# Moving the matmul operands of a three-stage transformer kernel to one address residue in SBUF

## The chip, the cores and the metric

The kernel runs on one core of one Trainium2 chip. The metric is the device time of one execution in microseconds (us). Before the change three runs gave 681.0, 681.89 and 684.74 us; the median is 681.89 us. A kernel computes on four engines with their own instruction queues: TensorE (PE, with its weight loads shown apart as PEld), VectorE (DVE), ScalarE (ACT) and GpSimd (POOL). SyncE (SP) issues the DMAs. SBUF is the on-chip memory from which TensorE reads both operands of a matmul; each of its 128 partitions holds a row of bytes, and "the address" below is the byte offset in that row.

## The reference

Attention with a local window and a few global columns (batch 2, 8 heads, 768 positions, head dimension 64), then two feed-forward stages on the 1536 x 512 result:

```python
scores = where(keep, q @ k.T / sqrt(64) - slope[h] * dist, -1e9)
x = softmax(scores) @ v              # reshaped to 1536 x 512
h = x @ w_in                         # 512 -> 2048
x = (h * cos(h)) @ w_out             # 2048 -> 512
return ((x @ w_a) * (x @ w_b)) @ w_out2   # 512 -> 1536 -> 512
```

The weights come as float64 and are converted on the chip.

## The kernel before

**Matmuls.** Each float32 operand is split into a high and a low part of type fp32r (xTh and xTl, wh and wl, gh and gl, yh and yl, ugh and ugl), and each product is made of three matmuls: high times high, high times low and low times high (lines 669 to 671 for h, a and b; 719 to 721 for y; 766 to 768 for o). Each takes a stationary operand of 128 columns, which a weight load brings into the array (512 bytes per partition), and streams a moving operand of 512 columns through it (2,048 bytes per partition). There are 2,448 such matmuls; the other 1,392 belong to attention (scores, transposes, weighing of v) and are shorter. For h the weights w are stationary and x moves; for y the weights are stationary and g moves; for a and b the weights are stationary and y moves; for o the product ug is stationary and the weights move.

**Stages.** The 1,536 rows are cut into three chunks of 512 (c = 0, 1, 2). Attention runs over 12 tiles of 128 rows, with the h and y work of the finished chunks between them; then h and y go on alone, then a, b and o. The order in which each engine gets its instructions is worked out by a planner (`Plan.order`, line 90) from costs and due times written in the file; it reads no addresses.

**Where tiles lie.** Tiles are allocated one after the other from pools, in this order: `const` (small constants), `keep` (the x and y tiles, and the accumulators acc0 to acc2), `wp` (converted weights, float64 buffers, and u and g tiles), and then `at` for attention, whose room is used afterwards by `post` (more weight and g tiles). Nearly every tile is a multiple of 256 bytes long, so its address modulo 256, the residue below, is that of the tile before it. The exceptions are what the change touches: the constants, which end at 1,856, and the float64 buffers of `RAW_BYTES` = 4,160 bytes (line 23), used in pairs inside the accumulators' room (line 579's `raws`, 2 x 4,160 bytes in each of acc0 to acc2) and singly as raw0 and raw1. The DMA of a weight block lands one byte into such a buffer, so that ScalarE and VectorE can pick bytes out of each float64.

Weight tiles wh and wl live in 17 numbered slots; slot 0 lies before raw0 and raw1, all others behind them.

Of the kernel before, what the change touches and what calls it, by code (L numbers as in the profile page):

```python
# [10 lines left out]
F32 = mybir.dt.float32  # L11
# [8 lines left out]
PSUM = bass.MemoryType.PSUM  # L20

P = 128
RAW_BYTES = 8 * 4 * P + 64
TOP = float(2.0**27)
GLOB = 32
BIG = float(2.0**40)
# [131 lines left out]
def tile_kernel(ctx, tc, q, k, v, n_global, n_local, w_in, w_out, w_a, w_b, w_out2, out):  # L158
# [11 lines left out]
    const = ctx.enter_context(tc.tile_pool(name="const", bufs=1))  # L170
# [41 lines left out]
    low_end = const.tile([P, 1], F32, tag="lowend", name="low_end")  # L212
    other = const.tile([P, 4], F32, tag="other", name="other")
    other_i = const.tile([P, 1], I32, tag="otheri", name="other_i")
    su = keep.tile([P, 2, 4, 2 * P], F32, tag="xh2", name="su")
    su_a, su_b = su[:, 0], su[:, 1]
    d = at.tile([P, H, 2, P], F32, tag="bias", name="bias")
# [340 lines left out]
    def weights():  # L558
        free = [(-1, s) for s in range(N_W[0])] + [(N_PRE, s) for s in range(N_W[0], sum(N_W))]
        free.sort()  # L560
        for n, blk in enumerate(sorted(first, key=lambda b: first[b])):
# [9 lines left out]
            def load(n=n, src=src, idx=idx, tiled=tiled, early=early):  # L571
                if early:
                    if n % 2 == 0:
                        T["raws", n // 2] = keep.tile([P, 2, RAW_BYTES], U8, tag=f"acc{n // 2}", name=f"raws{n // 2}")
                    T["raw", n] = T["raws", n // 2][:, n % 2]
                else:
                    T["raw", n] = wp.tile([P, RAW_BYTES], U8, tag=f"raw{n % 2}", name=f"raw{n}")
                block = src[idx] if tiled else src[idx * P:(idx + 1) * P, :]
# [356 lines left out]
```

## Time and profile before

| | before |
|---|---|
| median of three runs | 681.89 us |
| the profiled execution's own time | 682.8 us |
| its span, first to last instruction | 681.0 us |
| mean granted TensorE clock | 0.99 |
| PE busy / PEld busy | 96% / 79% of the span |
| DVE / ACT / POOL busy | 57% / 52% / 37% |
| 16 DMA engines, share of the span | 22.4% for the one large queue |

The profiled execution is 0.9 us longer than the median, and 1.8 us of its time lie outside the span. A matmul's recorded duration is modelled and overlaps the next matmul, so that the time one really takes is the distance from its start to the start of the next one, read from the timeline. Weight loads are recorded apart; a matmul's own load runs while the matmul before it streams.

### The profile page before, as it was taken

How to read it: one execution, taken by the hardware profiler on the slowest of the kernel's cores; microseconds unless marked ns; L12 is line 12 of the kernel's file. 1: busy time of each engine (PE TensorE's matmuls, PEld its weight loads, DVE VectorE, ACT ScalarE, POOL GpSimd, SP SyncE). 2: the span in 40 equal slices, each digit the busy share in tenths (PEclk: the TensorE clock that was granted, in tenths of full speed). 3: DMA queues.
4: the chain of work that ended last, by engine and by line, in shares of the span. 5: the costliest groups of instructions: out<-in, count | busy, mean ns of one | idle time of the engine just before them, and what ended most of it. 6: DMA issues, size and time to landing. Idle time of an engine off the chain costs nothing.

```text
span 681.0 us, 10027 instructions
## 1 busy us (share of the span) xinstructions
PE 653.7 (96%) x3840; PEld 535.6 (79%) x3840; DVE 388.9 (57%) x731; ACT 354.0 (52%) x621; POOL 253.2 (37%) x232
## 2 busy tenths in 40 slices
PE   3787999999999999999999999999999999999996
PEld 2676778888888888888888888888888888888885
DVE  6988888874877656665475555422552652322243
ACT  4878887866876755766565446411532532111100
POOL 5368773422433533545164235311521422211100
PEclk9988999999999999999999999999999999999999
DMA  7832241311122231213103313200220210000004
GB/s 212 288 88 77 78 127 43 82 42 32 63 93 93 93 124 62 94 63 123 63 31 100 117 36 121 92 1 0 93 92 1 94 62 1 0 1 1 0 34 158
DMA packets 29530, 50.63 MB, mean 74 GB/s; under 512 B 14944, under 2 KB 15776, under 8 KB 29472
## 3 DMA queue, kind: packets, MB, share of 16 engines
q1 hardware_dynamic: 29472, 49.89, 22.4%
q8 instruction: 32, 0.52, 0.3%
q14 instruction: 26, 0.21, 0.1%
HBM read 45.09 MB, written 3.15 MB: 71 GB/s over the span
## 4 chain that ended last, share of the span: by engine, by line
PE 92%; DVE 3%; issue 1%; DMA 1%; ACT 1%; POOL 1%; SPq 0%; DVEq 0%
PE h L669 7%; PE y L719 7%; PE y L721 6%; PE y L720 6%; PE h L670 6%; PE h L671 6%; PE a L670 5%; PE b L670 5%; PE a L669 5%; PE a L671 5%; PE b L671 5%; PE b L669 5%; PE o L767 5%; PE o L768 5%; PE o L766 5%; PE tr L191 3%
## 5 line engine op out<-in xcount | busy, mean ns | idle before, releaser
L194 POOL TENSOR_TENSOR wl<-cv,wh 128x512 fp32r<-128x512 f32 x59 | 79.5, 1351 | 127.8 <-ACT wh L200 127.8
L194 POOL TENSOR_TENSOR ugl<-as,ugh 128x512 fp32r<-128x512 f32 x36 | 47.9, 1331 | 164.5 <-ACT ugh L200 158.0
L754 DVE TENSOR_TENSOR as<-b,as 128x512 f32<-128x512 f32 x36 | 24.9, 691 | 124.6 <-ACT as L200 124.6
L200 ACT ACTIVATE as<-a 128x512 f32<-128x512 f32 x36 | 21.5, 597 | 132.5 <-PE a L671 132.4
L194 POOL TENSOR_TENSOR gl<-u,gh 128x512 fp32r<-128x512 f32 x48 | 64.2, 1353 | 62.7 <-ACT gh L200 57.2
L194 DVE TENSOR_TENSOR cv<-cv,cn 128x512 int32<-128x512 f32 x68 | 59.9, 881 | 32.7 <-ACT cv L586 32.4
L669 PE MATMUL h<-xTh,wh 128*128 128x512 f32 x192 | 76.4, 398 | 0.4 <-DVE u L708 0.4
L719 PE MATMUL y<-gh,wh 128*128 128x512 f32 x192 | 76.2, 397 | 0.0
L670 PE MATMUL h<-xTl,wh 128*128 128x512 f32 x192 | 75.6, 394 | 0.0
L671 PE MATMUL h<-xTh,wl 128*128 128x512 f32 x192 | 75.4, 393 | 0.0
L721 PE MATMUL y<-gh,wl 128*128 128x512 f32 x192 | 75.0, 391 | 0.0
L720 PE MATMUL y<-gl,wh 128*128 128x512 f32 x192 | 74.9, 390 | 0.0
L591 ACT ACTIVATE cn<-raw,low_end 128x512 f32<-128x512 int8 x62 | 47.0, 758 | 22.8 <-DVE cv L194 18.1
L780 DVE TENSOR_TENSOR oacc<-o,oacc 128x512 f32<-128x512 f32 x60 | 41.5, 691 | 27.1 <-PE o L768 26.3
L670 PE MATMUL a<-yl,wh 128*128 128x512 f32 x144 | 56.9, 395 | 0.0
L669 PE MATMUL a<-yh,wh 128*128 128x512 f32 x144 | 56.7, 394 | 0.0
L670 PE MATMUL b<-yl,wh 128*128 128x512 f32 x144 | 56.7, 394 | 0.0
L671 PE MATMUL a<-yh,wl 128*128 128x512 f32 x144 | 56.6, 393 | 0.0
L669 PE MATMUL b<-yh,wh 128*128 128x512 f32 x144 | 56.6, 393 | 0.0
L671 PE MATMUL b<-yh,wl 128*128 128x512 f32 x144 | 56.6, 393 | 0.0
L768 PE MATMUL o<-wh,ugl 128*128 128x512 f32 x144 | 56.3, 391 | 0.0
L767 PE MATMUL o<-wl,ugh 128*128 128x512 f32 x144 | 56.2, 390 | 0.0
(101 smaller groups left out, 1361.1 us busy)
## 6 DMA issues: line engine op xcount, KB each, us to landing
raw<-in_moe_w_out_dram SPq DMA_DIRECT2D x26, 512.0 KB, 3.3
raw<-in_moe_w_in_dram SPq DMA_DIRECT2D x12, 512.0 KB, 3.3
raw<-in_moe_w_a_dram SPq DMA_DIRECT2D x12, 512.0 KB, 3.2
raw<-in_moe_w_b_dram SPq DMA_DIRECT2D x12, 512.0 KB, 3.2
v<-in_v_dram SPq DMA_DIRECT2D x12, 256.0 KB, 3.9
out_dram<-oacc SPq DMA_DIRECT2D x12, 256.0 KB, 2.0
nq<-in_q_dram SPq DMA_DIRECT2D x11, 256.0 KB, 3.4
nk<-in_k_dram SPq DMA_DIRECT2D x11, 256.0 KB, 3.3
```

What stands on the lines that cost most here:

```text
L194: eng.tensor_tensor(out=dst, in0=a, in1=b, op=ALU.subtract)
L591: nc.scalar.activation(out=c, in_=top, func=AF.Relu, bias=low_end, scale=-TOP)
L669: nc.tensor.matmul(dst, wh[:, kk, :], xh[:, kk, :], start=(kk == 0), stop=False)
L670: nc.tensor.matmul(dst, wh[:, kk, :], xl[:, kk, :], start=False, stop=False)
L671: nc.tensor.matmul(dst, wl[:, kk, :], xh[:, kk, :], start=False, stop=(kk == KD - 1))
L719: nc.tensor.matmul(dst, wh[:, m, :], gh, start=(x == 0), stop=False)
L720: nc.tensor.matmul(dst, wh[:, m, :], gl, start=False, stop=False)
L721: nc.tensor.matmul(dst, wl[:, m, :], gh, start=False, stop=(x == L1[g] - 1))
L766: nc.tensor.matmul(dst, uh[:, us], wh, start=(x == 0), stop=False)
L767: nc.tensor.matmul(dst, uh[:, us], wl, start=False, stop=False)
L768: nc.tensor.matmul(dst, ul[:, us], wh, start=False, stop=(x == L2[g] - 1))
L780: nc.vector.tensor_tensor(out=acc, in0=T[inst], in1=acc, op=ALU.add)
```

## The change

Two lines give each buffer another size; no instruction is added, removed or moved. In the built programs each engine has the same instructions in the same order with the same waits, and only the addresses (and the length of a row in the raw buffers) differ.

```diff
-RAW_BYTES = 8 * 4 * P + 64
+RAW_BYTES = 8 * 4 * P + 256
...
     other = const.tile([P, 4], F32, tag="other", name="other")
     other_i = const.tile([P, 1], I32, tag="otheri", name="other_i")
+    const.tile([P, 8], F32, tag="pad", name="pad")
```

What this does to the addresses, read from the two built programs (address modulo 256):

```
tiles                                   before     after
xTh, yh of chunk 2 (tag xh2)              64         96
accumulators 0, 1, 2 (and raws)       64,192,64      96
xTh, yh of chunks 0, 1; xTl, yl of all   192         96
cv, cn; wh and wl of slot 0              192         96
raw0, raw1                             192, 0        96
wh and wl of slots 1 to 16                64         96
u, t, g, ug (high and low)                64         96
attention: kx 64, qT 96 and 160, sp 0, 160 and 192, pt 32 and 224:
                                 each 32 more; ident stays at 128
```

So before, a matmul's moving and stationary operands are either at the same residue (64 and 64, or 192 and 192) or 128 apart (64 and 192); counted over the built program, 1,076 of the 2,448 wide matmuls have their own two operands 128 apart. After, all 2,448 have both at 96, which is 32 modulo 64.

## Rows read from the trace of the kernel before

**Rows 1.** The page: busy shares, 40 slices, chain that ended last.

```profile
PE 653.7 (96%) x3840; PEld 535.6 (79%) x3840; DVE 388.9 (57%) x731; ACT 354.0 (52%) x621; POOL 253.2 (37%) x232
...
PE   3787999999999999999999999999999999999996
...
PEclk9988999999999999999999999999999999999999
...
PE 92%; DVE 3%; issue 1%; DMA 1%; ACT 1%; POOL 1%; SPq 0%; DVEq 0%
```

**Rows 2.** Busy time by stretch: us and instructions; PEclk is the granted clock.

```profile
core 0: us, PE busy (x) PEld busy (x) DVE busy (x) ACT busy (x) POOL busy (x), PEclk, DMA share, GB/s
153.10:674.50 521.40, 521.40 (x2269) 425.65 (x2268) 264.17 (x366) 236.42 (x381) 171.09 (x128) 1.00 0.18 62
...
60.00:153.00 93.00, 91.88 (x1075) 76.24 (x1073) 75.45 (x212) 74.73 (x142) 49.91 (x55) 1.00 0.26 72
```

**Rows 3.** PE's groups in 153.1 to 674.5: xcount | busy us, mean ns | idle before.

```profile
L719 PE MATMUL y<-gh,wh 128*128 128x512 f32 x164 | 64.0, 390 | 0.0
L721 PE MATMUL y<-gh,wl 128*128 128x512 f32 x164 | 63.9, 390 | 0.0
...
L670 PE MATMUL h<-xTl,wh 128*128 128x512 f32 x160 | 63.0, 394 | 0.0
...
L670 PE MATMUL a<-yl,wh 128*128 128x512 f32 x144 | 56.9, 395 | 0.0
...
L768 PE MATMUL o<-wh,ugl 128*128 128x512 f32 x143 | 55.9, 391 | 0.0
```

**Rows 4.** Timeline of PE: start us, duration us; first matmul of successive runs.

```profile
343.32 0.39 PE L719 MATMUL y<-gh,wh 128*128 128x512 f32 x1
...
359.64 0.40 PE L669 MATMUL b<-yh,wh 128*128 128x512 f32 x1
...
362.43 0.40 PE L669 MATMUL a<-yh,wh 128*128 128x512 f32 x1
...
365.23 0.40 PE L669 MATMUL b<-yh,wh 128*128 128x512 f32 x1
...
368.03 0.40 PE L669 MATMUL a<-yh,wh 128*128 128x512 f32 x1
```

**Rows 5.** Timeline of PE, two runs of h of 12 matmuls, y between them.

```profile
285.57 0.39 PE L669 MATMUL h<-xTh,wh 128*128 128x512 f32 x1
...
288.30 0.39 PE L719 MATMUL y<-gh,wh 128*128 128x512 f32 x1
...
291.02 0.40 PE L669 MATMUL h<-xTh,wh 128*128 128x512 f32 x1
291.03 0.19 PEld L670 LDWEIGHTS h<-xTl,wh 128*128 128x128 f32 x1
...
293.82 0.39 PE L719 MATMUL y<-gh,wh 128*128 128x512 f32 x1
```

**Rows 6.** Timeline, the last run of o and what follows it.

```profile
647.62 0.39 PE L766 MATMUL o<-wh,ugh 128*128 128x512 f32 x1
...
674.59 0.39 PE L768 MATMUL o<-wh,ugl 128*128 128x512 f32 x1
675.02 0.69 DVE L780 TENSOR_TENSOR oacc<-o,oacc 128x512 f32<-128x512 f32 x1 [0.67 <-PE o L768]
```

**Rows 7.** Tiles sp, qT, wh, nk and raw: durations min/median/max in ns.

```profile
L191 PEld LDWEIGHTS tr<-ident,sp x176: 137/141/230, 13.1 to 148.3; 128*128 128x128 f32 x176
...
L378 PEld LDWEIGHTS sc<-kx,qT x288: 182/185/336, 6.0 to 133.2; 64*128 64x128 f32 x144
...
L669 PEld LDWEIGHTS h<-xTh,wh x192: 186/188/192, 62.5 to 342.4; 128*128 128x128 f32 x192
...
L197 POOL TENSOR_SCALAR kx<-nk x9: 614/618/623, 9.9 to 120.8; 128x512 fp32r<-128x512 f32 x9
...
L586 ACT ACTIVATE cv<-raw,low_end x62: 734/752/774, 75.0 to 578.4; 128x512 f32<-128x512 int8 x62
```

**Rows 8.** Timeline of PE: one run over v in attention.

```profile
130.80 1.40 PE L426 MATMUL o<-v,pt 128*128 128x65 bf16 x40
132.04 0.52 PE L191 MATMUL tr<-ident,sp 128*128 128x128 f32 x3
```

## The prediction

> **What bounds the kernel now.** I began with the page [rows 1]. PE is busy for 96% of the span, its slices stand at 9 from the fifth of the forty to the last but one, and the chain that ended last is PE for 92%: the reader should see that from there on the kernel lasts as long as PE takes to get through its matmuls. The granted clock is at its upper level, 2.4 GHz, in nearly every slice, so the clock is not what can change. Next came the stretches [rows 2]: from 153.1 to 674.5 us PE is busy in all of 521.40 us, while DVE, ACT and POOL are busy for 264, 236 and 171 us. In the same stretch PE's groups show no idle time before them [rows 3]; their counts (492 for y, 480 for h, 432 each for a and b, 431 for o) add up to 2,267 wide matmuls. That is 521.4 / 2,267 = 230.0 ns for one, at a clock at which 512 columns need 213.3 ns. So each matmul takes some 17 ns more than its columns, with nobody to wait for. Attention, before 153 us, is a mixture: PE is nearly full there too (91.88 of 93 us from 60 us on), but among short matmuls and waits.
>
> Then I asked whether the 230 ns are the same everywhere, by the starts in the timeline. A run of 72 matmuls of y takes from 343.32 to 359.64 us, 226.7 ns each; the four runs of 12 that follow it, b, a, b, a, take 2.79 or 2.80 us each, 232.5 to 233.3 ns [rows 4]. In y both operands lie at residue 64; in those a and b runs y (192) moves against weights at 64. The last 120 matmuls of o, both operands at 64, start from 647.62 to 674.59 us: 226.6 ns over 119 distances [rows 6]. This might be a matter of the line instead of the address, so the decisive pair is one line with two addresses [rows 5]: the h run at 285.57 us has its weights in slot 0, both operands at 192, and takes 2.73 us for 12 (227.5 ns, its last matmul already beside a load from 64); the h run at 291.02 us has the same kind of x at 192 and weights at 64, and takes 2.80 us (233.3 ns). Equal residues at 64 and at 192 are alike, unequal ones cost about 6 ns more. The weight load of the next matmul starts 0.01 us after the matmul that it runs beside [rows 5], so the pair that counts should be a moving operand and the next stationary one.
>
> **The change part by part.** It issues nothing new and moves nothing past a queue, no wait is added, and planner and DMAs stay as they are. Three things change: the relation of the two PE operands, the common residue of both, and where all other engines and the DMAs find their tiles.
>
> First the relation. By the addresses, 1,012 of the 2,267 matmuls in the full stretch run beside a load from the other residue. After the change none does. If every matmul then took the 226.7 ns of the equal runs, the stretch would need 2,267 x 0.2267 = 513.9 us, some 7.6 us less than the 521.56 us from 153.03 to 674.59 us. Not all equal runs reach the floor: the slot 0 run stands at 227.5 ns. I take 227.0 ns, which makes 514.6 us and a gain of 6.9 us. By another way, 1,012 x 6.3 ns (233.0 less 226.7) is 6.4 us, and the rest of the 7.6 us is from equal pairs between unequal ones. The bounds are 6.4 and 7.6 us. All of it is on the path, since PE waits for nothing in the stretch; what is late next would be the eviction of the last bank and its DMA behind 674.59 us [rows 6], which simply start earlier by as much. For the others to become the bound PE would have to wait: DVE, the busiest of them, fills 51% of the stretch, and PE's demand rises by 1.3%.
>
> Before 153 us 83 wide matmuls have unequal pairs: 83 x 6.3 ns = 0.5 us, of which waits of attention will swallow some; between 0 and 0.5 us I take 0.3 us. In attention the distances between the operands' residues stay, since all of its tiles move by 32 together; only the transposes' ident stays at 128 while sp and xn move by 32. Loads of sp at 0, 160 and 192 have one median, 141 ns, with 137 as the least [rows 7], so I put that at nothing.
>
> Second the common residue, 96. Both equal cases of the trace are at 0 modulo 64, and no 512-column stream of it starts at 32 modulo 64; this price is not shown. Nearest rows: weight loads at 32 modulo 64 (qT, all 288 of them) have a median of 185 ns and loads at 0 modulo 64 (wh) 188 ns [rows 7], so half a block of 64 bytes makes a load no longer. Among moving operands only v starts at both kinds of place: 40 short matmuls of 64 or 65 columns take 1.24 us together [rows 8], 31 ns each, against 26.7 ns for 64 columns at 2.4 GHz; whatever a bad start costs there is within those 4 ns. The bound above is therefore one more 64-byte block of 33 for a 2,048-byte stream, 226.7 / 32 = 7.1 ns or 16.1 us over 2,267 matmuls; below nothing, a residue that costs less than 64 does, where the 13.4 ns above the columns are the most that can go, though no row shows even one of them going. I take zero, as the loads and v are nearest to it, and keep -3 and +16 us for the tails.
>
> Third the other engines. POOL reads nk at residues 64 and 96 in turn, and its nine copies last 614 to 623 ns; ACT reads raw0 at 192 and raw1 at 0, and its 62 conversions lie between 734 and 774 ns with a median of 752 [rows 7]. Nothing there goes by the address, and from 153 us on none of it is on the path. Cost zero; if that cover were gone, the 20 ns by which such rows spread, on perhaps 100 instructions of attention's path, would be 2 us either way.
>
> The sum is -6.9 - 0.3 = -7.2 us: 682.8 less 7.2 is 675.6 us for an execution like the profiled one. That one lies 0.9 us above the median of the runs, 681.89 us, which goes to **674.7 us**.
>
> The Trainium skill speaks against this gain: "TensorE: Matmul & The Clock Gate", section "Step-by-step: what each phase is for", gives TensorE two independent SBUF read ports, one for the streaming operand and one for the weight load. By that rule the place of one cannot slow the other, and the change would be worth nothing; rows 4 and 5 disagree with it, with 226.7 against 233.3 ns. The same page's "Back-to-back issue gap" gives N/2.4 + 2.5, 215.8 ns for 512 columns; no run of the trace is that short, so it is no floor to reckon with.
>
> **The rivals.** (1) *Relation without effect*: what I read as addresses goes by something that comes with them (the tile, the stage, the neighbours), and nothing changes: 681.9 us. For it: nearly all unequal pairs are in h, a and b, nearly all equal ones in y and o. Against it: the two h runs of rows 5.
>
> (2) *Half a block more*, the case on the other side: a stream that starts at 32 modulo 64 touches 33 blocks where it touched 32, and PE pays for the block on each of the 2,267 matmuls. At 7.1 ns it costs 16.1 us, the equal residues still give back 7.2, and the time is 681.9 + 16.1 - 7.2 = 690.8 us. It decides against the change from 3.2 ns per matmul on (7.2 us / 2,267). For it: no wide stream of the trace starts there. Against it: qT's loads and v.
>
> (3) *Half of the gain*: the floor at 96 lies half way between 227.0 and the 230.0 ns of now, at 228.5 ns: 2,267 x 1.5 ns = 3.4 us are lost again, which leaves 678.1 us. For it: 227.5 ns in rows 5. Against it: 226.7 ns over 72 and over 119 matmuls.
>
> (4) *A cheaper residue*: a part of the 13.4 ns goes, say 1.5 ns each: 671.3 us. Nothing in the trace speaks for it but that 96 has not been seen.
>
> **How the numbers follow.** The forecast's own case (673.5 to 676.5 us) gets 0.70, rival 1 0.08, rival 2 0.10, rival 3 0.09, rival 4 0.03. The range leaves out rival 2 and most of rival 4, and reaches up to rivals 3 and 1: 671.8 to 682.0 us. Half a per cent, 3.4 us, is about what a measurement can tell from no change; 678.5 us is therefore the edge of faster. Faster: 0.70 + 0.03 + half of rival 3, 0.78. Same: the other half, rival 1 and a mild form of rival 2, 0.13. Slower: 0.09.
>
> **What would show it.** Right: in the changed kernel's timeline the runs of a, b and h take the same 2.72 us per 12 matmuls as y and o, about 226.7 ns from start to start, and the stretch from the end of attention to the last matmul is about 7 us shorter, with PE busy throughout and the durations of DVE, ACT and POOL as before. Rival 1 is shown by a and b runs still at 2.80 us while y stays at 2.72; rival 2 by y and o runs that are longer than before, 2.81 us for 12 or more; rival 3 by all runs near 2.74 us. The prediction is wrong if the relation of the two residues is not what sets the distance, or if a common residue of 96 has a floor of its own above 228 ns; also if PE begins to show idle time after 153 us.

## The result, and the profile after

The changed kernel takes 675.83 us (median of six runs, 674.37 to 676.8), the kernel before 683.55 us (median of six, the three shown before and three more): 7.7 us less, a ratio of 0.9892 with a 95% interval of 0.987 to 0.9914. The forecast was 674.7 us and 7.2 us less. The profiled execution takes 675.8 us with a span of 674.0, where before had 682.8 and 681.0.

The page of the changed kernel answers to [rows 1]; PE is busy for 6.6 us less, its weight loads for 1.1 us more, and DVE, ACT and POOL for as long as before, to 0.3 us.

```profile
PE 647.1 (96%) x3840; PEld 536.7 (80%) x3840; DVE 388.6 (58%) x731; ACT 354.0 (53%) x621; POOL 253.0 (38%) x232
...
PE   4787999999999999999999999999999999999996
...
PEclk9987999999999999999999999999999999999998
...
PE 92%; DVE 4%; DMA 1%; issue 1%; POOL 1%; ACT 1%; SPq 0%; DVEq 0%; POOLq 0%
```

The stretch from the end of attention to the last matmul, by window and by PE's groups, answers to [rows 2, 3] (columns as there; all lines stand one further down):

```profile
153.60:667.50 513.90, 513.90 (x2270) 425.69 (x2268) 264.44 (x366) 236.42 (x381) 171.02 (x128) 1.00 0.18 63
```

```profile
L720 PE MATMUL y<-gh,wh 128*128 128x512 f32 x164 | 63.9, 390 | 0.0
...
L671 PE MATMUL h<-xTl,wh 128*128 128x512 f32 x160 | 62.3, 389 | 0.0
...
L671 PE MATMUL a<-yl,wh 128*128 128x512 f32 x144 | 56.0, 389 | 0.0
...
L769 PE MATMUL o<-wh,ugl 128*128 128x512 f32 x143 | 55.6, 389 | 0.0
```

The same 2,267 matmuls, with no idle time before them, take 513.9 us instead of 521.4 (the counts of the windows include records that reach over their edges), and the mean record, 390 to 395 ns before, is 389 or 390 ns for every group. DVE, ACT and POOL are busy for as long as before (264, 236 and 171 us). The timeline shows it without any model in between; these are the starts that answer to [rows 4]:

```profile
341.40 0.39 PE L720 MATMUL y<-gh,wh 128*128 128x512 f32 x1
...
357.72 0.39 PE L670 MATMUL b<-yh,wh 128*128 128x512 f32 x1
...
360.44 0.39 PE L670 MATMUL a<-yh,wh 128*128 128x512 f32 x1
...
363.16 0.39 PE L670 MATMUL b<-yh,wh 128*128 128x512 f32 x1
...
365.88 0.39 PE L670 MATMUL a<-yh,wh 128*128 128x512 f32 x1
```

The 72 matmuls of y take 16.32 us as before; b, a and b take 2.72 us for 12, not 2.79 or 2.80. The two runs of h that answer to [rows 5], 2.73 and 2.80 us before, take 2.72 us each, and so does the y between them:

```profile
284.28 0.39 PE L670 MATMUL h<-xTh,wh 128*128 128x512 f32 x1
...
287.00 0.39 PE L720 MATMUL y<-gh,wh 128*128 128x512 f32 x1
...
289.72 0.39 PE L670 MATMUL h<-xTh,wh 128*128 128x512 f32 x1
...
292.44 0.39 PE L720 MATMUL y<-gh,wh 128*128 128x512 f32 x1
```

The last run of o and the eviction behind it [rows 6] begin 7.0 us earlier and are otherwise unchanged:

```profile
640.60 0.39 PE L767 MATMUL o<-wh,ugh 128*128 128x512 f32 x1
...
667.57 0.39 PE L769 MATMUL o<-wh,ugl 128*128 128x512 f32 x1
667.99 0.69 DVE L781 TENSOR_TENSOR oacc<-o,oacc 128x512 f32<-128x512 f32 x1 [0.67 <-PE o L769]
```

From 153.59 to 667.57 us the stretch is 513.98 us long, 7.58 us less than the 521.56 us before. The span fell by 7.0 us only, since attention ended at 153.59 us instead of 153.03. That half microsecond goes with the clock in this execution; here is the granted clock (the 1.00 column) around 60 us, first before, then after:

```profile
50.00:55.00 5.00, 3.59 (x62) 2.96 (x58) 3.76 (x13) 4.39 (x9) 4.59 (x5) 1.00 0.08 29
55.00:60.00 5.00, 2.95 (x25) 2.67 (x26) 4.96 (x13) 3.37 (x8) 2.88 (x4) 0.67 0.68 183
60.00:65.00 5.00, 5.00 (x63) 4.28 (x61) 3.86 (x13) 4.56 (x9) 5.00 (x6) 0.99 0.00 0
```

```profile
50.00:55.00 5.00, 2.67 (x50) 2.17 (x48) 3.88 (x14) 5.00 (x11) 4.92 (x5) 1.00 0.19 34
55.00:60.00 5.00, 3.20 (x29) 2.91 (x30) 4.14 (x11) 2.69 (x6) 3.28 (x5) 0.56 0.63 161
60.00:65.00 5.00, 5.00 (x54) 4.30 (x52) 3.96 (x10) 3.96 (x9) 3.21 (x5) 0.76 0.00 0
```

PE had waited for 2.87 us (before) and 3.54 us (after) ahead of 57 us, and its clock fell to the lower level, 1.2 GHz (0.50 granted from 57 to 60 us in both). After the change it stayed there longer: between 60 and 65 us 0.76 of full speed was granted instead of 0.99, and fewer matmuls got through. The scores behind the wait start 0.25 us earlier than before (56.80 against 57.05 us), the first wide matmul of h 0.87 us later (63.39 against 62.52 us). In another execution of the changed kernel (e7 below) attention ended at 152.7 us.

### The profile page after: what moved, and what is told of

The parts are those of the page before. It is cut to its first block, busy times and chain, and to the rows that moved or that the text cites. A ratio compares the mean times of both kernels' runs of the same rounds, so it can differ in the third digit from the quotient of the medians.

```text
span 674.0 us, 10027 instructions
## 1 busy us (share of the span) xinstructions
PE 647.1 (96%) x3840; PEld 536.7 (80%) x3840; DVE 388.6 (58%) x731; ACT 354.0 (53%) x621; POOL 253.0 (38%) x232
## 4 chain that ended last, share of the span: by engine, by line
PE 92%; DVE 4%; DMA 1%; issue 1%; POOL 1%; ACT 1%; SPq 0%; DVEq 0%; POOLq 0%
PE y L720 7%; PE h L670 7%; PE y L722 6%; PE y L721 6%; PE h L672 6%; PE h L671 6%; PE a L672 5%; PE b L672 5%; PE o L768 5%; PE o L769 5%; PE b L671 5%; PE a L671 5%; PE o L767 5%; PE a L670 5%; PE b L670 5%; PE tr L191 4%
## 5 line engine op out<-in xcount | busy, mean ns | idle before, releaser
L767 PE MATMUL o<-wh,ugh 128*128 128x512 f32 x144 | 56.0, 389 | 0.0
```

Of the source, the lines that this page charges most:

```text
L767: nc.tensor.matmul(dst, uh[:, us], wh, start=(x == 0), stop=False)
```

## The experiments

**e1: all wide operands at 64.** Only the buffers are padded:

```diff
-RAW_BYTES = 8 * 4 * P + 64
+RAW_BYTES = 8 * 4 * P + 256
```

Expected:

> Only the float64 buffers are padded, the constants not: all wide operands lie at 64 modulo 256 instead of 96. Theory (what counts is that the moving operand and the next stationary one have the same residue): 226.7 ns from start to start in y, h, a, b and o alike, ratio to before 0.989 +- 0.003. Rival (the residue 96 itself is cheaper or dearer than 64): another floor than 226.7 ns, 2,267 matmuls long, 2.3 us for each ns.

Measured: 0.9905 (0.9875 to 0.9936). PE's stretch:

```profile
154.70:668.60 513.90, 513.90 (x2269) 425.54 (x2268) 264.53 (x366) 236.38 (x381) 171.08 (x128) 1.00 0.19 63
```

From its first to its last matmul it is 513.97 us long, against 513.98 us of the changed kernel. Both do the same: the 32 bytes of padding in the constants bring nothing there and cost nothing.

**e2: only the constants padded.**

```diff
     other_i = const.tile([P, 1], I32, tag="otheri", name="other_i")
+    const.tile([P, 8], F32, tag="pad", name="pad")
```

Expected:

> Only the constants are padded: every tile lies 32 bytes further than before, and 1,076 wide matmuls still have their operands 128 apart. Theory: nothing is gained, ratio to before 1.000 +- 0.003, the stretch after attention 521.5 us as before, a and b with chunks 0 and 1 at 2.80 us for 12. Rival (32 modulo 64 is by itself the better start): a gain of some us.

Measured: 1.0008 (0.9988 to 1.0028).

```profile
153.30:674.80 521.50, 521.50 (x2269) 425.65 (x2268) 264.28 (x366) 236.41 (x381) 171.10 (x128) 1.00 0.19 62
```

The stretch is 521.57 us long, as before. So the whole gain is that of the other edit.

**e3: x and y 128 bytes away from the weights.** The changed kernel with one more line:

```diff
     const.tile([P, 8], F32, tag="pad", name="pad")
+    wp.tile([P, 32], F32, tag="pad2", name="pad2")
```

Expected:

> The changed kernel with 128 bytes of padding ahead of the wp pool: x and y stay at 96, weights and g lie at 224. All of h, a and b (1,344 matmuls of the stretch after attention) have operands 128 apart, y and o the same residue. Theory: h, a and b go back to 232.5 to 233.3 ns, y and o stay at 226.7 ns; 1,344 x 6.3 ns = 8.5 us more than the changed kernel, ratio to before 1.001 (0.997 to 1.005). Rival (the lines h, a and b had gained by something else, as the raw buffers' rows): they stay at 226.7 ns, ratio 0.989.

Measured: 1.0044 (1.0025 to 1.0063), slower than the kernel before. Its timeline has these starts, 12 matmuls from each to the next:

```profile
361.39 0.40 PE L671 MATMUL b<-yh,wh 128*128 128x512 f32 x1
...
364.19 0.40 PE L671 MATMUL a<-yh,wh 128*128 128x512 f32 x1
...
366.99 0.40 PE L671 MATMUL b<-yh,wh 128*128 128x512 f32 x1
...
369.79 0.40 PE L671 MATMUL a<-yh,wh 128*128 128x512 f32 x1
...
372.58 0.39 PE L721 MATMUL y<-gh,wh 128*128 128x512 f32 x1
...
375.32 0.39 PE L721 MATMUL y<-gh,wh 128*128 128x512 f32 x1
...
378.04 0.39 PE L721 MATMUL y<-gh,wh 128*128 128x512 f32 x1
```

b and a are back at 2.79 and 2.80 us for 12 with the raw buffers as in the changed kernel; the rival falls. In the mean h, a and b take 233.0 ns, 1,344 x 6.3 = 8.5 us, as forecast. The stretch is 523.29 us long, 9.3 us more than the changed kernel's. The other 0.8 us is in y and o, 227.6 ns instead of 226.7, though their own operands lie at the same residue: the first 12 of the y run above take 2.74 us, the next 12 take 2.72 us. Something of the run before them stays with the first few matmuls.

**e4: a map.** Nothing but matmuls on two tiles, 12 of each kind in a row:

```python
N_EACH = 12
...
    for rm in range(0, 256, 32):
        for rs in range(0, 256, 32):
            add(f"grid {rm} {rs}", [(rm, rs)] * N_EACH)
...
                nc.tensor.matmul(banks[n % 8][:wide, :cols], b[:, s // size:s // size + wide], a[:, m // size:m // size + cols],
                                 start=(x == 0), stop=(x == len(pairs) - 1))
```

Each pair is (moving byte, stationary byte). Behind the grid come smaller groups with other distances, narrower stationary operands, fewer columns and 16-bit types.

Expected:

> Not the reference's work: 1,644 matmuls on two fixed tiles and nothing else, in groups of 12 with one moving and one stationary address each. Theory: 226.7 ns where the two addresses are equal modulo 256, 233 ns at 128 apart, whatever the common residue; in between some curve of the distance. If the extra 13.3 ns over 512 columns are due to the weight load that runs beside the stream, they shrink with a narrower stationary operand (6.7 ns at 64 columns) and stay as many ns for a stream of 256 columns. Rival: they belong to the matmul itself, and stay for narrow loads.

Measured, as the mean ns from start to start inside each group without its first distance (from the records' starts; rows: residue of the moving operand, columns: of the stationary one):

```
          0     32     64     96    128    160    192    224
  0   226.7  233.1  233.3  234.0  231.6  233.7  229.2  233.2
 32   233.4  228.9  233.1  233.3  234.0  231.6  233.7  229.2
 64   228.6  233.2  226.6  233.1  233.3  234.0  231.7  233.7
 96   233.2  228.9  233.2  226.7  233.1  233.3  234.0  231.6
128   233.3  233.8  229.1  233.2  226.7  233.0  233.4  234.0
160   234.6  233.3  233.8  229.1  233.2  226.7  233.1  233.4
192   233.4  234.0  231.7  233.8  229.1  233.2  226.7  233.0
224   232.2  233.3  234.0  231.7  233.7  229.2  233.1  226.6
```

The table goes by the difference of the two residues: 0 gives the least (but for 32 and 32, to which e8 comes back), moving 64 ahead of stationary gives 229, the others 232 to 235. Further steps of 256 bytes, up to 3,840, change nothing (227.1 to 227.7 with difference 0, 232.8 or 232.9 with 128).

The part of the expectation on the cause failed: with a stationary operand of 64 or 32 columns the distance was 230.4 to 231.5 ns instead of shrinking, so the 13.3 ns over the columns do not go by the columns that are loaded. With fewer columns streamed the extra stays, but the relation no longer tells: at 256 columns the mean is 119.4 ns with difference 0 and 118.7 ns with 128 (12.7 and 12.0 over 106.7), at 384 columns it is 176.3 and 176.0 ns (some 16 over 160). Groups of bf16 by fp16 operands took 215.9 ns with the moving operand at each of the four residues tried, 2.6 ns over the columns. They also read half the bytes, so whether the type or the bytes set the extra is not shown.

**e5: every 4 bytes.** The same with 64 differences:

```python
for d in range(0, 256, 4):
    add(f"d {d}", [(d, 0)] * 18)
...
add("own next", [(0, 128 * (n // 2 % 2)) for n in range(48)])
```

Expected:

> Not the reference's work: again only matmuls on two fixed tiles, 18 of each kind. The moving operand lies d bytes behind the stationary one, d from 0 to 252 in steps of 4. Theory: the least is at d = 0, 226.7 ns, and the rest lies between 228 and 240 ns, so that the changed kernel already has the best relation. Rival: another distance gives less than 226 ns, and a kernel with its wide operands at that distance would beat both. Where a moving operand stays at 0 and the stationary one turns between 0, 0, 128, 128: by the prediction's reading (the next load counts) the matmuls of own 0 and next 128, and of own 128 and next 128, are the slow ones; if own and next both count, three of four are.

Measured: the means lie between 226.6 and 240.0 ns, none below 226.6. The floor is reached at difference 0 and also at 28, 60, 108, 236 and 240 (226.6 to 227.0), and 156 and 252 end on it after two and four matmuls; all differences that are 4 modulo 16 give 233 to 240. No other distance beats the changed kernel's, so there is no version to make of it. The turning stationary operand contradicts both readings that were to be told apart: the distances of one kind of pair alternate, 235 and 227 ns for own 0 and next 0, 230 and 240 ns for own 128 and next 128. A matmul's distance is thus not a price of its pair alone. Nor is difference 0 the best for a narrower load: in eight further groups with a stationary operand of 64 columns the distance was 230.2 ns at difference 0, 230.2 to 231.6 at six others, and 226.6 at 160.

**e6: 64 ahead, in the kernel**, and **e7: the changed kernel again** beside it. e6 is e3 with another length:

```diff
+    wp.tile([P, 48], F32, tag="pad2", name="pad2")
```

Expected of e6, then of e7:

> The changed kernel with 192 bytes of padding ahead of the wp pool: x and y stay at 96, weights and g lie at 32 modulo 256, so that in h, a and b the moving operand is 64 ahead of the stationary one. Theory (the map of distances holds in the kernel): h, a and b at about 229 ns, y and o at 226.7 ns; 1,344 x 2.2 ns = 3.0 us more than the changed kernel, ratio to before 0.994. Rival (only equal residues are cheap in the kernel, every other distance costs like 128): 233 ns, ratio 1.003.

> The changed kernel once more, beside the one above: ratio to before 0.989 (0.987 to 0.991), the stretch after attention 514.0 us; the end of attention moves by up to 2 us from execution to execution.

Measured: e7 0.9901 (0.9868 to 0.9934) with a stretch of 513.98 us once more, e6 1.0005 (0.9987 to 1.0023) with 520.73 us. That is 6.75 us more than the changed kernel, where 3.0 were expected. The starts of e6, 12 matmuls from each to the next:

```profile
366.58 0.39 PE L671 MATMUL a<-yh,wh 128*128 128x512 f32 x1
...
369.32 0.39 PE L671 MATMUL b<-yh,wh 128*128 128x512 f32 x1
...
372.07 0.39 PE L671 MATMUL a<-yh,wh 128*128 128x512 f32 x1
...
374.82 0.40 PE L721 MATMUL y<-gh,wh 128*128 128x512 f32 x1
...
377.59 0.39 PE L721 MATMUL y<-gh,wh 128*128 128x512 f32 x1
```

a and b take 2.74 or 2.75 us, 229 ns, as the map says; over the stretch h, a and b have a mean of 229.6 ns, 1,344 x 2.9 = 3.9 us. The miss is in y and o, whose operands have the same residue, 32: the first 12 after a run of a take 2.77 us, 231 ns, and the starts come every 226.7 ns only from the eleventh on. y and o mostly come 12 at a time, so only the last two of a run get there; their mean is 229.8 ns, 923 x 3.1 = 2.9 us.

**e8: long runs.** To tell settling from a price of the residue, 72 matmuls of each kind behind 12 with 128 between the operands:

```python
for r in (0, 32, 96, 16, 48, 4, 100):
    add(f"reset {r}", [(128, 0)] * 12)
    add(f"both {r}", [(r, r)] * 72)
...
```

Expected:

> Not the reference's work: matmuls on two fixed tiles, each kind 72 times behind 12 with the operands 128 apart. Theory (equal residues settle at 226.7 ns after some matmuls, whatever the common residue, and the map's 228.9 ns at 32 and 32 were the settling): both at 0, 32, 96, 16, 48, 4 and 100 all end at 226.7 ns. Rival (the common residue has to be a multiple of 32): 0, 32 and 96 end there, 16, 48, 4 and 100 stay at 230 to 238 ns. 64 and 128 apart stay at 229 and 233 ns.

Measured in windows inside the runs, in the order 0, 32, 96, 16, 48, 4, 100:

```profile
28.00:42.00 14.00, 14.00 (x63) 11.59 (x63) 0.00 (x0) 0.00 (x0) 0.00 (x0) 1.00 0.00 0
47.50:61.00 13.50, 13.50 (x61) 11.21 (x60) 0.00 (x0) 0.00 (x0) 0.00 (x0) 1.00 0.01 1
67.00:80.00 13.00, 13.00 (x59) 10.74 (x58) 0.00 (x0) 0.00 (x0) 0.00 (x0) 1.00 0.00 0
86.00:99.50 13.50, 13.50 (x60) 10.99 (x59) 0.00 (x0) 0.00 (x0) 0.00 (x0) 1.00 0.00 0
105.50:119.00 13.50, 13.50 (x60) 10.99 (x59) 0.00 (x0) 0.00 (x0) 0.00 (x0) 1.00 0.01 1
125.00:138.50 13.50, 13.50 (x59) 10.73 (x58) 0.00 (x0) 0.00 (x0) 0.00 (x0) 1.00 0.00 0
145.00:158.50 13.50, 13.50 (x58) 10.73 (x57) 0.00 (x0) 0.00 (x0) 0.00 (x0) 1.00 0.00 0
```

In 13.5 us 61 matmuls are touched at 32, 60 at 16 and 48, and 58 or 59 at 4 and 100. By the starts, 0, 32 and 96 settle at 226.7 ns (0 and 96 after three matmuls, 32 after nine), 16 and 48 stay at 231.1 ns and 4 and 100 at 237.8 ns. The rival is right on the residue, the theory on the settling: equal is not enough, and the map's 228.9 ns at 32 and 32 was settling. Of the differences tried in the same way, 28, 60 and 156 settle at 226.7 ns too. Where a run starts from matters besides: both operands at 48 gave 233.0 ns in groups of 18 in e5 and 231.1 ns here, difference 240 gave 226.6 ns in e5 and 236.7 ns here, 108 gave 226.9 and 233.3 ns, and even the runs with 128 between keep two rhythms, 238 and 229 in turn in some and a cycle of seven from 228 to 241 in others.

## Why the prediction was right, and where its steps were not

**The relation of the two operands** was the right cause; e1 and e2 show that the gain belongs to the edit that makes the residues equal, e3 that it goes when h, a and b are made unequal again, and rival 1 falls. Its term was forecast as 6.9 us, with 6.4 and 7.6 as bounds, and measured as 7.58, the upper bound itself. What was mis-sized was the floor: I took 227.0 ns for each matmul because a run with equal residues stood at 227.5 ns [rows 5]. By its starts that run takes 231 ns first, then 226 or 227, and 228 and 232 at its end, where the loads from 64 come; the y matmul ahead of it, beside a load from 192, takes 232. So its slow distances lie next to the unequal pairs, and e8 shows such a settling by itself. Where all are equal nothing has to settle, and the mean over all 2,267 is 226.72 ns. The bound worked out from the 72 and 119 long runs [rows 4, 6] would have been the better value.

**"The pair that counts should be a moving operand and the next stationary one"** failed as a mechanism. It fitted the mixed pairs that the prediction had looked at, but e5 has one pair at two distances in turn, and e3 and e6 have equal pairs that are slow behind unequal ones. What the runs show instead is a rhythm of PE's stream that settles, mostly within ten matmuls, on the floor or on a slower cycle. Why equal addresses settle on the floor was not shown. The sum did not need it, since after the change both readings make all pairs equal.

**The common residue, 96, costs nothing**: right here, 513.98 us against 513.97 us at 64 (e1), and with it rivals 2 (690.8 us), 3 (678.1 us) and 4 (671.3 us) fall. But the reason given, that weight loads and the short reads of v do not care, would have let through 16 or 4 as well, and e8 shows 231.1 and 237.8 ns there. Over 2,267 matmuls that would by estimate have been 10 and 25 us. So rival 2 had the right worry, a start that costs, with the wrong step: all eight multiples of 32 below 256 reach the floor (e4, e8), and the four starts tried between them, 4, 16, 48 and 100, do not. That 96 is one of the good ones was luck, as far as the reason given goes.

**The other engines and the DMAs, zero**: right in the stretch after attention. POOL's copies of nk have a median of 620 ns (618 before), the conversions of raw 752 ns as before [rows 7], and the busy times in the stretch are the same to 0.3 us.

**Attention, 0.3 us less**: it was 0.56 us more in the profiled execution, with the clock shown above; in the seven profiles of the whole kernel in this study its end lies between 152.6 and 156.7 us, so nothing of this size can be told there from one profile. The stretch behind attention repeats to 0.01 us (513.98 us in both profiles of the changed kernel), so the runs of one kernel should differ mostly by the rest; this is not shown, since only one run of each was traced.

**The rule on two independent read ports**, under the Trainium skill's "TensorE: Matmul & The Clock Gate", "Step-by-step: what each phase is for", by which the change was worth nothing, does not describe these matmuls of 512 columns: their distances lie between 226.6 and 240 ns by the two addresses and what ran before (e4, e5). With 256 and 384 columns the one difference tried cost nothing (e4).

**The time itself**, 675.83 us against 674.7 us, is off by 1.1 us because the starting point moved: the three runs shown before had a median of 681.89 us, and with three more, of 683.22 to 684.12 us, it is 683.55 us. The difference, 7.7 us, is 0.5 us more than forecast.

## What to carry to other kernels

Where a long stretch of fp32r matmuls runs without idle time, divide it by their number and compare runs of the same length in the timeline; 3% between lines that do the same work is not noise. Where they stream 512 columns against loads of 128, lay out SBUF so that every operand which TensorE streams and every one that it loads start at the same residue modulo 256, a multiple of 32, and beware of one odd-sized buffer in front of the others. Since a few matmuls after each unequal one are slow too, it pays to make all of them equal, not most. For shorter streams or narrower loads these runs show no such gain (e4, e5).

## What the runs showed of the hardware that was not expected

With 512 columns a stream of fp32r matmuls takes 226.7 ns each at best, 13.3 ns over the columns at 2.4 GHz; a bf16 by fp16 matmul takes 215.9 ns at each of four places of its moving operand (e4). The extra does not shrink with a narrower load, and it does not grow in proportion to the columns: it is some 12 to 13 ns at 256 columns and 16 at 384, where 128 bytes between the operands cost nothing. At 512 columns the penalty of a bad relation has a memory: behind unequal ones, equal residues took three matmuls to settle at 0, 96 and 224, and nine or ten at 32 (e3, e6, e8). That is not a matter of the residue alone: at 0 it took ten behind loads of 64 columns (e5, the last group).
